# Products of 448 features as pairs of 64-row matmuls in two jobs, in a new order of all jobs

## The chip, the cores and the metric

The kernel runs on one core of a Trainium2 chip. Its engines work side by side: TensorE multiplies (PE in the profile, its weight loads PEld), VectorE (DVE) and ScalarE (ACT) do the elementwise work, GpSimd (POOL) some small things, and SyncE (SP) issues most of the DMAs. The metric is the device time of one execution in microseconds (us), the median of several runs.

## The reference, cut to what matters

```python
# x [2048, 448], H = 16 heads of 28, window W = 8 at dilation 2
h  = x + attention(layernorm(x) @ wqkv) @ wo      # each query sees 8 keys: pos, pos-2, .. pos-14
z  = gelu(layernorm(h) @ w_in)                    # [2048, 1792]
z1, z2 = z[:, :896], layernorm(z[:, 896:])
g  = w_sp @ z2 + b_sp[:, None]                    # [2048, 2048] times [2048, 896]
h2 = h + (z1 * g) @ w_out
```

All inputs and the result are bf16. Four of these products contract over 448 features: with wqkv (in the kernel qk and v), wo (y) and w_in (z1 and z2). 448 is three and a half times the 128 rows of TensorE.

## The kernel before

Every piece of work is a job of the `Planner`: a name, an engine, its operations with what they read and write, and a ticket for one or two of the eight PSUM banks where it needs them. `order` (line 301) doesn't plan. It puts the jobs in the order of the hand-written list ORDER (line 26), whose numbers are the jobs in the order of their creation, and gives each ticket the banks of the list BANK. `Sched.issue` (line 148) then goes through this order, works out which semaphores each operation has to wait for, and appends it to its engine's queue; every engine runs its own queue strictly in that order. A wait of TensorE on TensorE is left out there, since its matmuls end in order. So what is before what on one engine is read from ORDER alone, and the interleaving of different engines in it means nothing by itself. ON says which copies out of PSUM run on ACT, DVE or POOL.

The jobs on TensorE, by name:

- `warm`, the filler: one matmul of 256 columns on constant data. It stands in ORDER as many times as wanted, here only ahead of the first products.
- `xT0` to `xT3`: transposes of the first four normalised blocks of 128 tokens, copied out by `xe`. The other blocks are transposed by DMA.
- `qk t_g`: queries and keys of token range t (QT, two ranges of 256 tokens and three of 512) and head group g; weights `wqk`, which `wp` copies spread out of `wraw` (loads `wq_0` to `wq_4`), each head padded to 32 columns; copied out by `qe`.
- `v b`: values of two blocks of the attention; copied out by `ve`. 448 columns.
- `lg b_j`: logits of one block and half of the heads, 8 matmuls of 28 rows; `ex` takes the exponential on ACT, `mk` applies the mask on DVE.
- `o b`: probabilities times values, 16 matmuls of 29 columns; `rc`, `om`, `od` normalise, `oT` transposes by DMA.
- `y m`: the output projection of two token blocks; `h` adds it to x; `st1`, `mv1`, `rs1`, `n1` are the second layer normalisation, and `hT` transposes by DMA into hnT.
- `z2_m` (448 columns) and `z1_u` (512 columns): the two halves of the product with w_in; `z2c` copies raw, `z2g` and `z1g` take the gelu on ACT, and `st2`, `mv2`, `rs2`, `n2` normalise z2 on DVE and POOL.
- `g fc_tc_q`: four matmuls of 512 columns of the product with w_sp, of 16 that add up in one bank (line 958); `ua` and `um` on DVE add b_sp and multiply by z1.
- `wo m`: the product with w_out (line 982); `r` adds h on DVE and `out` stores. The last block, 15, is done in two halves of 224 columns.

The products with 448 features all go through `product` (line 485). It makes a job "F" (two, F0 and F1, for qk of the first range and for v0) of six matmuls with all 128 rows, three for each of two results in two banks (FK), and a job "H" of the half chunks (HK): one matmul with rows 0 to 63 for the first result and one with rows 64 to 127 for the second (`tile_position` (0, 0) and (64, 0)). The rows of the half chunk are taken so that the two matmuls lie on different rows and in different banks. F and H of one product stand anywhere in ORDER, in either order, and any of them may come first in its bank.

Of the kernel before, what the change touches and what calls it, by code (L numbers as in the profile page):

```python
# [6 lines left out]
D = 448  # L7
# [18 lines left out]
ORDER = [1, 25, 115, 26, 40, 2, 921, 921, 10, 921, 39, 30, 921, 921, 9, 31, 921, 921, 8, 27, 921, 41, 921, 5, 921, 43, 921, 6,  # L26
# [40 lines left out]
BANK = [2, 1, 5, 4, 0, 2, 6, 4, 6, 2, 0, 2, 4, 4, 2, 0, 0, 2, 4, 6, 6, 0, 4, 0, 4, 6, 4, 6, 0, 6, 7, 2, 0, 2, 2, 4, 6, 4, 3,  # L67
# [65 lines left out]
class Sched:  # L133
# [14 lines left out]
    def issue(self, exe, fn, reads=(), writes=(), dma=False):  # L148
# [23 lines left out]
        for e, c in sorted(needed.items(), key=lambda t: -t[1]):  # L172
# [8 lines left out]
            if c > myvc.get(e, 0):  # L181
                myvc[e] = c
# [138 lines left out]
def bass_sequential_preLN__sliding_local_dilated__mixer_gmlp__prompt_kernel(  # L321
# [17 lines left out]
    with contextlib.ExitStack() as top:  # L339
# [380 lines left out]
        def values(b):  # L720
# [12 lines left out]
            if b == 0:  # L733
                rd = [W_v + xh_res(k0, k0 + NK) for k0 in k0s]
# [320 lines left out]
```

## Time and profile before

| | |
|---|---|
| median of 3 runs | 240.5 us (240.25 to 240.63) |
| span of the profiled execution, first to last instruction | 238.8 us |
| TensorE busy | 232.1 us |
| DVE, ACT, POOL busy | 150.4, 91.6, 32.5 us |
| TensorE's first filler, first transpose, first product, first spatial matmul | at 1.51, 6.20, 8.88 and 118.16 us |

The profile is one execution of the program. Its own time outside of the profiler isn't known; the span leaves out what lies before the first and after the last instruction. Matmuls are pipelined: each row of TensorE has a modelled end, so rows overlap, and the distance from one start to the next is the better measure of what a matmul costs. A few records of matmuls are missing from the trace. In the rows below, L499 is the matmul of `product`, L797 the logits, L821 probabilities times values, L958 the spatial product, L982 the output, L660 the transposes and L997 the filler.

### The profile page before, as it was taken

What the parts mean: (1) busy time and instruction counts of PE and PEld (TensorE: products, weight loads), DVE (VectorE), ACT (ScalarE), POOL (GpSimd) and SP (SyncE); (2) the same over time, 40 slices, a digit from 0 to 9 for tenths busy, and PEclk for the clock granted to TensorE, in tenths of its full rate; (3) what the DMA queues carried; (4) which work ended last, traced back from release to release, by engine and by line L of the source; (5) the groups of instructions that cost most, each with busy time, mean ns of one, the idle gap of its engine ahead of it and who ended that gap; (6) DMA issues with size and microseconds to landing.
All of it is one profiled execution on the core that took longest, in us unless ns stands there. A gap on an engine that the chain in (4) does not pass through costs nothing.

```text
span 238.8 us, 4201 instructions
## 1 busy us (share of the span) xinstructions
PE 232.1 (97%) x1706; PEld 114.1 (48%) x1723; DVE 150.4 (63%) x321; ACT 91.6 (38%) x112; POOL 32.5 (14%) x75
## 2 busy tenths in 40 slices
PE   7899999999999999999999999999999999999995
PEld 5665445445455544444444444444444444444462
DVE  5899986999988985499985045024522514422863
ACT  3788487878889874679730000000000000000000
POOL 4450120320402121103242000000000000000000
DMA  5952424565852696999999990000000000003012
GB/s 139 337 166 55 91 53 91 137 170 148 112 103 47 119 149 133 186 148 200 192 235 182 160 198 3 0 3 0 0 0 21 3 0 19 0 3 115 19 58 77
DMA packets 66553, 23.10 MB, mean 97 GB/s; under 512 B 58726, under 2 KB 66406, under 8 KB 66534
## 3 DMA queue, kind: packets, MB, share of 16 engines
q1 hardware_dynamic: 66464, 22.83, 45.6%
q8 instruction: 13, 0.21, 0.4%
q14 instruction: 6, 0.05, 0.1%
q10 hardware_dynamic: 70, 0.00, 0.0%
HBM read 6.72 MB, written 1.84 MB: 36 GB/s over the span
## 4 chain that ended last, share of the span: by engine, by line
PE 94%; DMA 2%; SPq 1%; issue 1%; DVE 0%; DVEq 0%
PE psum L958 40%; PE psum L499 40%; PE psum L982 9%; PE psum L821 3%; PE psum L797 3%; DMA wraw<-in_A_wqkv_dram 2%; SPq L530 1%; DVE srg L989 0%; DVE wqk L515 0%; DVEq L203 0%
## 5 line engine op out<-in xcount | busy, mean ns | idle before, releaser
L967 DVE TENSOR_TENSOR ub<-psum,bb 128x512 bf16<-128x512 f32 x28 | 19.2, 690 | 53.8 <-PE psum L958 53.5
L958 PE MATMUL psum<-wsp_hi,z2p 128*128 128x512 bf16 x218 | 49.3, 379 | 0.3
L806 ACT ACTIVATE E<-psum 128x896 bf16<-128x896 f32 (+2 forms) x36 | 31.9, 928 | 6.8 <-PE psum L797 6.8
L958 PEld LDWEIGHTS psum<-wsp_hi,z2p 128*128 128x128 bf16 x224 | 21.9, 98 | 26.1
L499 PE MATMUL psum<-xhT,wqk 128*128 128x512 bf16 (+3 forms) x154 | 26.8, 336 | 1.0 <-issue 0.6
L958 PE MATMUL psum<-wsp_lb,z2p 128*128 128x512 bf16 x110 | 25.9, 379 | 0.2
L958 PE MATMUL psum<-wsp_la,z2p 128*128 128x512 bf16 x109 | 25.6, 379 | 0.3 <-issue 0.2
L499 PE MATMUL psum<-w_in,hnT 128*128 128x448 bf16 (+1 forms) x128 | 25.4, 353 | 0.1
L499 PE MATMUL psum<-hnT,w_in 128*128 128x512 bf16 (+1 forms) x112 | 24.4, 379 | 0.0
L982 PE MATMUL psum<-w_out,z1p 128*128 128x448 bf16 (+1 forms) x119 | 22.7, 341 | 0.0
L812 DVE TENSOR_TENSOR E<-E,maskb 128x1792 bf16<-128x1792 bf16 (+2 forms) x18 | 19.5, 1098 | 0.4 <-ACT E L806 0.4
L620 DVE BATCH_NORM_STATS2 st<-x_tm 128x6 f32<-128x448 bf16 x32 | 18.6, 608 | 1.7 <-DMA x_tm<-in_A_x_dram 1.6
L884 DVE BATCH_NORM_STATS2 st<-z2p 128x6 f32<-128x448 bf16 x32 | 18.4, 607 | 1.9 <-ACT z2p L877 1.6
L989 DVE TENSOR_TENSOR srg<-psum,x_tm 128x448 bf16<-128x448 f32 (+1 forms) x17 | 9.9, 594 | 13.2 <-PE psum L982 7.3
L499 PEld LDWEIGHTS psum<-xhT,wqk 128*128 128x128 bf16 (+1 forms) x160 | 12.3, 96 | 11.3 <-issue 2.5
L615 POOL TENSOR_TENSOR rs<-rs,negh 128x2 f32<-128x2 f32 (+1 forms) x21 | 17.2, 820 | 1.8
L958 PEld LDWEIGHTS psum<-wsp_lb,z2p 128*128 128x128 bf16 x112 | 10.9, 98 | 13.2
L958 PEld LDWEIGHTS psum<-wsp_la,z2p 128*128 128x128 bf16 x112 | 10.9, 98 | 13.4 <-DVE st L884 0.4
L925 ACT ACTIVATE z1p<-psum 128x1024 bf16<-128x1024 f32 x14 | 14.0, 1022 | 6.8 <-PE psum L499 6.8
L982 PEld LDWEIGHTS psum<-w_out,z1p 128*128 128x128 bf16 x119 | 11.6, 98 | 10.1
L499 PEld LDWEIGHTS psum<-w_in,hnT 128*128 128x128 bf16 (+1 forms) x128 | 10.3, 97 | 12.2 <-issue 3.2
L499 PEld LDWEIGHTS psum<-hnT,w_in 128*128 128x128 bf16 (+1 forms) x112 | 9.1, 96 | 11.2 <-issue 1.9
(54 smaller groups left out, 221.3 us busy)
## 6 DMA issues: line engine op xcount, KB each, us to landing
w_in<-in_B_w_in_dram SPq DMA_DIRECT2D x8, 224.0 KB, 3.0
out_dram<-srg SPq DMA_DIRECT2D x16, 112.0 KB, 1.7
x_tm<-in_A_x_dram SPq DMA_DIRECT2D x3, 448.0 KB, 5.9
w_out<-in_B_w_out_dram SPq DMA_DIRECT2D x1, 784.0 KB, 5.8
bb<-in_B_b_sp_dram SPq DMA_DIRECT2D x1, 512.0 KB, 5.5
wraw<-in_A_wqkv_dram SPq DMA_DIRECT2D x1, 448.0 KB, 4.7
wv<-in_A_wqkv_dram SPq DMA_DIRECT2D x2, 224.0 KB, 5.6
wo<-in_A_wo_dram SPq DMA_DIRECT2D x1, 336.0 KB, 5.8
```

The source lines that it names most:

```text
L499: ins = e.matmul(o, w, x, start=g not in seen, stop=left[g] == 0, **kw)
L615: (lambda e: e.tensor_tensor(R, A, negh[:, 0:1].to_broadcast([128, n]), ALU.pow), [rr, r_negh], r_rs[k][m:m + n])],
L620: [(lambda e: e.bn_stats(st[:, m, :], src), [rsrc], [r_st[k][m]])], dve_t(D))
L797: ins = e.matmul(psum[:, c:c + nq], qkT[p:p + DH, 2 * g + 1, k0:k0 + NK], qkT[p:p + DH, 2 * g, t0:t0 + nq], start=True, stop=True, tile_po ...
L806: return e.activation(o, i, AF.Exp, scale=SCALE)
L812: return e.tensor_tensor(a, a, maskb[:, 0:1, pad:pad + nq].to_broadcast([NK, NHEAD, nq]), ALU.mult)
L884: [(lambda e, m=m, k=k: e.bn_stats(st3[:, m, k, :], z2p[:, m, D * k:D * (k + 1)]), [r_z2[m]], [r_st[2][m]])], dve_t(D))
L925: return e.activation(o, i, AF.Gelu_apprx_tanh)
L958: ins = e.matmul(psv(tk), z2p[:, s, 128 * fc:128 * fc + 128], w[:, 512 * (tc % 2):512 * (tc % 2) + 512], start=(s == 0), stop=(s == NB - 1))
L967: [(lambda e, tc=tc, s=s, tk=tk: e.tensor_tensor(ub[:, s, :], psv(tk), bb[:, 512 * tc:512 * tc + 512], ALU.add), [r_bb], [r_ub[s]])], dve_ ...
L982: ins = e.matmul(psv(tk, 0, c1 - c0), z1p[:, fc, 128 * m:128 * m + 128], w_out[:, fc, c0:c1], start=(fc == 0), stop=(fc == FC7 - 1))
L989: [(lambda e, m=m, s=s, tk=tk, c0=c0, c1=c1: e.tensor_tensor(srg[:, s, c0:c1], psv(tk, 0, c1 - c0), x_tm[:, m, c0:c1], ALU.add), [r_x[m]], ...
```

## The change

`product` now makes fourteen matmuls of 64 rows for two results k of 448 features: the four chunks of the features are cut into lower (rows 0 to 63) and upper halves (64 to 127), three and a half chunks for each result. They are issued as pairs, a lower half for one result next to an upper half for the other. Job "A" holds four pairs, with the first result on the lower and the second on the upper rows; job "B" holds three pairs the other way round. A comes first, and B waits on TensorE's own semaphore for the end of A (`own`), since the two results change rows and both add up in the same banks. At least one other job of TensorE must lie between (`apart`).

```diff
+        def product(name, key, out, w, x, n, tk, reads, low=LOW, upp=UPP):
+            def pair(kl, ku):
+                return [e for a, b in zip([(kl, 0, c) for c in low[kl]], [(ku, 64, c) for c in upp[ku]]) for e in (a, b)]
+            first = [(0, 0, low[0][0]), (1, 64, upp[1][0])]
+            last = [(1, 0, low[1][-1]), (0, 64, upp[0][-1])]
+            def f(e, part):
+                for k, p0, c in part:
+                    ins = e.matmul(out(k), w(k, p0, c), x(k, p0, c), start=(k, p0, c) in first, stop=(k, p0, c) in last, tile_position=(p0, 0))
                 return ins
...
+            pa, pb = pair(0, 1), pair(1, 0)
+            ja = pl.job(name + "A", "pe", key, [(lambda e: f(e, pa), reads(pa), [])], 4 * half_t(n), acq=tk, kind="H")
+            jb = pl.job(name + "B", "pe", key, [(lambda e: f(e, pb), reads(pb), [])], 3 * half_t(n), acq=tk, kind="H")
+            pl.apart.append((ja, jb))
...
+LOW = [(0, 3, 2, 1), (0, 3, 1)]
+UPP = [(0, 3, 2), (0, 3, 1, 2)]
...
     def issue(...)
+        if own is not None:
+            waits.append(("pe", own))
...
     def order(self):
+        line = [j for j in out if j.eng == "pe"]
+        for a, b in self.apart:
+            between = line[line.index(a) + 1:line.index(b)]
+            assert between, ("no job between the two halves", a.name)
+            self.own[b] = a
```

ORDER, BANK and ON are new lists. Some dependencies that were written out (`after=` for logits, values, z1 and z2 and several loads, and `hold` for the loads of w_in) are gone; the lists alone set those orders now. TensorE's part of ORDER, written out by names up to the spatial product, before:

```
22*warm xT0 2*warm xT1 4*warm xT3 xT2 qk0_2F0 qk0_1F1 qk0_2F1 qk0_1F0 qk0_1H qk0_2H qk0_0H qk0_3H qk0_0F0 qk0_0F1
qk0_3F0 qk0_3F1 qk1_3F qk1_3H qk1_0H lg1_0 lg0_1 qk1_0F qk1_1F qk1_2F lg0_0 qk1_2H qk1_1H v0H v0F1 v0F0 lg1_1 lg2_0
v2F lg3_1 lg3_0 v2H v4F o0 o1 lg2_1 v4H qk2_0H qk2_0F qk2_3F qk2_2F qk2_1F qk2_2H v6H qk2_3H qk2_1H v6F o2 lg4_1 lg6_0
o3 qk3_3F lg4_0 lg5_1 qk3_3H qk3_2H qk3_2F lg5_0 lg6_1 qk3_1H qk3_1F v8F o5 o4 v8H y0H y0F lg7_1 lg7_0 qk3_0F lg8_0
lg8_1 qk3_0H qk4_0H qk4_0F o6 o7 qk4_1F lg10_0 lg10_1 qk4_1H y2H y2F v10H lg11_1 lg11_0 v10F o8 y4F lg9_1 lg9_0 y4H
qk4_2H qk4_2F lg12_1 lg12_0 qk4_3F o11 o9 o10 qk4_3H v16H v16F v12F lg13_1 lg13_0 v14H v12H v14F y6F lg15_0 lg14_1 y6H
z2_1H z2_1F o13 o12 z2_3H lg17_0 lg15_1 z2_3F y8F lg17_1 lg16_0 y8H z2_2H z2_2F z2_5H lg14_0 lg16_1 z2_5F o15 z1_0F
o14 z1_0H y10H z2_0H y10F z2_0F o17 o16 z1_1F z2_4F z1_1H z2_4H y12H y12F z1_2F z2_6F z2_6H z1_5H z2_7H z1_2H z1_5F
z2_7F z1_4F z1_6F y14F y14H z1_4H z1_6H z2_10H z2_10F z2_11F z1_9F z2_9F z2_13H z2_11H z2_9H z1_9H z2_13F z1_7F z2_12H
z2_8H z1_7H z1_8H z2_8F z1_8F z2_12F z1_12F z2_15F z1_12H z1_10H z2_14H z2_15H z1_10F z2_14F z1_11F z1_3F z1_13F
z1_11H z1_13H z1_3H g4_0_0 g3_0_0 g1_0_0
```

and after:

```
42*warm xT0 xT1 5*warm xT2 3*warm xT3 4*warm qk0_0A qk0_3A qk0_1A qk0_0B qk0_3B qk0_1B qk1_2A qk1_0A qk1_2B qk1_3A
qk0_2A qk1_0B qk0_2B qk1_1A qk1_3B qk1_1B lg0_0 v0A lg2_0 lg0_1 v0B v2A lg3_1 v2B lg3_0 lg2_1 v4A lg1_0 lg1_1 v4B
qk2_2A qk2_1A qk2_3A qk2_1B qk2_0A qk2_2B qk2_3B qk2_0B v6A o1 o0 lg4_0 lg4_1 v6B o2 qk3_2A lg6_1 lg5_0 qk3_2B qk3_3A
o4 lg5_1 lg6_0 o3 qk3_3B qk3_0A lg8_0 lg7_1 qk3_0B v8A qk3_1A lg8_1 lg7_0 v8B qk3_1B v10A o6 o5 v10B y0A lg9_1 lg9_0
y0B qk4_0A o7 lg11_0 lg10_1 o8 qk4_0B y2A lg12_1 lg10_0 y2B qk4_1A qk4_3A lg11_1 lg12_0 qk4_3B qk4_1B y4A qk4_2A y4B
qk4_2B v12A o10 o9 lg13_1 lg13_0 v12B o11 y6A lg14_0 lg15_1 y6B v14A lg15_0 v14B v16A lg14_1 lg16_0 v16B z2_0A o12 o13
lg17_1 z2_0B z2_1A lg17_0 lg16_1 z2_1B y8A z2_3A z2_2A z1_1A z2_3B y8B z2_2B z1_1B o14 o15 o16 o17 z2_4A z2_5A z2_4B
z2_5B y10A z1_0A y10B z1_0B z2_7A z1_4A y12A z2_7B y12B z1_4B z1_5A z2_6A z1_3A z2_6B z1_3B z2_9A z1_5B y14A z2_9B
y14B z2_8A z1_2A z1_6A z2_8B z1_2B z2_11A z1_9A z2_10A z2_11B z1_9B z1_6B z1_8A z1_7A z2_10B z1_7B z1_8B z2_13A z2_12A
z2_13B z2_14A z2_12B z2_14B z2_15A z1_10A z2_15B z1_12A z1_11A z1_13A z1_10B z1_13B z1_12B z1_11B g2_1_0 g3_0_0 g4_0_0
```

From there on TensorE has the same jobs g and wo in another order; before, the last were wo15 (two halves), wo12, wo14, wo13, and now they are wo13, wo12, wo14, wo15. SP's loads begin, before, with x0 x1 x2 wq_4 wq_3 wq_0 wq_1 wq_2 x4 wv_0 x8 wv_1 wo_1 wo_0 x12 wo_2, and after with x0 wq_4 x1 x2 x8 wq_1 x12 wq_3 wq_0 wq_2 x4 wo_2 wlo1 wv_1 wv_0; x8, x12, x4 and wq_0 have 448 KB each, x2 and the two wv 224, x0, x1, wq_1 and wq_4 112, wq_2 and wq_3 56. DVE casts wp0_0, wp2_0, wp3_1 first before, and wp3_1, wp0_0, wp4_2 after. Among the copies, z2c13 and ve12 go from DVE to ACT. In DVE's queue the normalisations n2_0 to n2_3 have two statistics (st2) of other blocks behind them after, and nine before.

More of the change, by code (lines that the diff above doesn't have):

```diff
@@ L146, in __init__, with issue @@
         self.store_keys = []
-    def issue(self, exe, fn, reads=(), writes=(), dma=False):
+    def issue(self, exe, fn, reads=(), writes=(), dma=False, own=None):
         prod, inc = exe, 1
@@ L233, in __init__ @@
         self.tickets = []
+        self.apart = []
         self.filler = None
@@ L292, in job @@
         return j
-    def hold(self, j, first):
-        if first not in j.deps:
-            j.deps.add(first)
-            j.ndep += 1
-            first.succ.append(j)
     def order(self):
@@ L756, in project @@
             tk = Ticket(2)
[L758 to L763 removed]
+            product("y%d" % m, key, lambda i, tk=tk: psv(tk, i, D), lambda i, p0, c, m=m: otv(64, p0, c, m + i),
+                    lambda i, p0, c: wo[p0:p0 + 64, c, :], D, tk, lambda part: r_wo2 + rot, LOWY, UPPY)
             pl.job("h%d" % m, "dve", kh,
@@ L800, in f @@
                     return ins
-                lgs[(b, j)] = pl.job("lg%d_%d" % (b, j), "pe", b + KEY["lg"], [(f, rq, [])], 0.2, acq=tk, kind="L", after=[o_jobs.get(b - NE)])
+                lgs[(b, j)] = pl.job("lg%d_%d" % (b, j), "pe", b + KEY["lg"], [(f, rq, [])], 0.2, acq=tk, kind="L")
                 def f2(e, nq=nq, j=j, slot=slot, tk=tk):
@@ L855, in bass_sequential_preLN__sliding_local_dilated__mixer_gmlp__prompt_kernel @@
         last_exp = exps[(NAB - 1, 1)]
-        gate = [lgs[(NAB - 1, 1)]]
         for m in range(NB):
             tk = Ticket(2)
-            def f(m=m, tk=tk):
-                return (
-                    [(k, psv(tk, k, D), hnT[:, m, FK[k][i], :], w_in[:, FK[k][i], FH + D * k:FH + D * (k + 1)], None)
-                     for i in range(3) for k in range(2)],
-                    [(k, psv(tk, k, D), hnT[p0:p0 + 64, m, c, :],
-                      w_in[p0:p0 + 64, c, FH + D * k:FH + D * (k + 1)], (p0, 0)) for k, (c, p0) in enumerate(HK)])
             kz = KEY["zr"] + KEY["zrs"] * m if RAW2[m] else KEY["z2"] + KEY["z2s"] * m
-            product("z2_%d" % m, kz, f, r_wi + [r_hn[m]], D, 6, tk, [] if RAW2[m] else gate)
+            product("z2_%d" % m, kz, lambda k, tk=tk: psv(tk, k, D), lambda k, p0, c, m=m: hnT[p0:p0 + 64, m, c, :],
+                    lambda k, p0, c: w_in[p0:p0 + 64, c, FH + D * k:FH + D * (k + 1)], D, tk, lambda part, m=m: r_wi + [r_hn[m]])
             def out2(m=m):
@@ L905, in bass_sequential_preLN__sliding_local_dilated__mixer_gmlp__prompt_kernel @@
             tk = Ticket(2)
-            def f(pair=pair, tk=tk):
-                return (
-                    [(i, psw(tk, i), w_in[:, c, 128 * fc:128 * fc + 128], hnT[:, 4 * tc:4 * tc + 4, c, :], None)
-                     for i, (fc, tc) in enumerate(pair) for c in FK[i]],
-                    [(i, psw(tk, i), w_in[p0:p0 + 64, c, 128 * fc:128 * fc + 128],
-                      hnT[p0:p0 + 64, 4 * tc:4 * tc + 4, c, :], (p0, 0)) for i, ((fc, tc), (c, p0)) in enumerate(zip(pair, HK))])
             rh = []
@@ L915, in bass_sequential_preLN__sliding_local_dilated__mixer_gmlp__prompt_kernel @@
                 rh += r_hn[4 * tc:4 * tc + 4]
-            product("z1_%d" % u, KEY["z1"] + KEY["z1s"] * u, f, r_wi + rh, 512, 6, tk, gate)
+            product("z1_%d" % u, KEY["z1"] + KEY["z1s"] * u, lambda i, tk=tk: psw(tk, i),
+                    lambda i, p0, c, pair=pair: w_in[p0:p0 + 64, c, 128 * pair[i][0]:128 * pair[i][0] + 128],
+                    lambda i, p0, c, pair=pair: hnT[p0:p0 + 64, 4 * pair[i][1]:4 * pair[i][1] + 4, c, :], 512, tk, lambda part, rh=rh: r_wi + rh)
             def f2(e, pair=pair, tk=tk):
@@ L927, in bass_sequential_preLN__sliding_local_dilated__mixer_gmlp__prompt_kernel @@
                    after=[last_exp], tbl="gelu")
-        for i, j in enumerate(j_win):
-            pl.hold(j, o_jobs[WINB + i])
-        load("bb", lambda: bb[:], lambda: B_b_sp.rearrange("(o n) -> o n", o=1).to_broadcast([128, S_TOK]), [r_bb], 0.6, (1.4, 3.2), key=28.0,
-             after=[o_jobs[NAB - 1]])
-        wl_ev = [o_jobs[min(b, NAB - 1)] for b in range(19)] + [j for j in ht_jobs for _ in range(2)]
-        late = ht_jobs[-1]
+        load("bb", lambda: bb[:], lambda: B_b_sp.rearrange("(o n) -> o n", o=1).to_broadcast([128, S_TOK]), [r_bb], 0.6, (1.4, 3.2), key=28.0)
         for s in range(NB):
@@ L1011, in bass_sequential_preLN__sliding_local_dilated__mixer_gmlp__prompt_kernel @@
                     reads += brs
-                key = sch.issue(j.eng, fn, reads, writes, dma=len(op) > 3)
+                key = sch.issue(j.eng, fn, reads, writes, dma=len(op) > 3, own=ends[pl.own[j]] if j in pl.own else None)
+                if j.eng == "pe":
+                    ends[j] = sch.cnt["pe"]
                 if j.name.startswith("out") or j.name == "touch":
```

86 lines of the change are left out of this document (25 added, 61 removed), and 100 rows, old and new, of tables (BANK, ON, ORDER).

## The prediction

> **What bounds the kernel now.** I read the head of the page and its chain of work first, then the waits of TensorE, then its timeline piece by piece.
>
> ```profile
> span 238.8 us, 4201 instructions
> ...
> PE 94%; DMA 2%; SPq 1%; issue 1%; DVE 0%; DVEq 0%
> ```
>
> ```profile
> PE psum L997 <- DVE warm L589: 1.5, 1, 1.5
> PE psum L499 <- issue: 0.6, 4, 0.2
> PE psum L660 <- DVE xn L631: 0.6, 2, 0.3
> PE psum L499 <- DVE wqk L515: 0.2, 1, 0.2
> PE psum L958 <- issue: 0.2, 1, 0.2
> ```
>
> The chain is TensorE's own work (94%). Its waits are over before 9.4 us, but for five of 0.16 us with no releaser, where the count of a row is one matmul short: a missing record and no wait. So from the first product to the last matmul the time is the sum of what TensorE executes, and only three things can move it: when the first product starts, what the stream costs, and what follows the last matmul. Next, the price of each kind, in start us, length, instruction, count:
>
> ```profile
> 86.54 0.38 PE L499 MATMUL psum<-hnT,w_in 64*128 64x512 bf16 x2
> 86.76 0.35 PE L499 MATMUL psum<-w_in,hnT 64*128 64x448 bf16 x2
> 86.95 1.78 PE L499 MATMUL psum<-hnT,w_in 64*128 64x512 bf16 x8
> 88.56 1.30 PE L499 MATMUL psum<-w_in,hnT 128*128 128x448 bf16 x6
> 89.70 2.75 PE L499 MATMUL psum<-hnT,w_in 128*128 128x512 bf16 x12
> 92.29 1.59 PE L499 MATMUL psum<-wo,OT 128*128 128x448 bf16 x8
> 93.72 0.59 PE L499 MATMUL psum<-hnT,w_in 64*128 64x512 bf16 x4
> 94.15 2.73 PE L499 MATMUL psum<-w_in,hnT 64*128 64x448 bf16 x14
> ```
>
> Starts count, since the lengths overlap. Six full matmuls of 448 columns last 88.56 to 89.70, 0.189 each; twelve of 512 last 2.59, 0.216 each. A pair of 64-row matmuls behind another pair costs the same as one full matmul: 0.22 for 512 columns (86.54 to 86.76), 0.19 for 448 (86.76 to 86.95). A change between full and half rows costs about 0.107: the eight at 92.29 are six full ones and a pair, seven passes or 1.32, and last 1.43; the eight at 86.95 are a pair and six full ones, 1.51, and last 1.61.
>
> ```profile
> 17.89 0.40 PE L797 MATMUL psum<-qkT 28*128 28x112 bf16 x16
> 18.22 1.31 PE L499 MATMUL psum<-wv,xhT 128*128 128x448 bf16 x6
> ...
> 21.23 0.95 PE L821 MATMUL psum<-V,E 128*128 128x29 bf16 x32
> 22.12 0.37 PE L797 MATMUL psum<-qkT 28*128 28x112 bf16 x8
> 22.42 0.36 PE L499 MATMUL psum<-wv,xhT 64*128 64x448 bf16 x2
> ```
>
> The logits are a third mode of 28 rows. Two jobs in a row (x16) take 0.33 us, and one alone (x8) takes 0.30: a run of logits costs some 0.33 whether it holds one job or two, and 0.10 more to enter it.
>
> **The change part by part.** *The products.* There are 67 of them. Each had six full matmuls and one pair; now it has seven pairs. Both are seven passes, and by the rows above a pass costs the same, so the stream itself gains and loses nothing: 89.1 us for the products (56 passes of 256 columns at 0.109, 182 of 512, 231 of 448), 96.7 for 448 spatial matmuls, 21.2 for the output, 7.3 for 18 attention jobs (0.40 each: 0.89 for two at 21.23 less a drain), 214.2 in all.
>
> *The changes of mode.* I wrote TensorE's part of ORDER out by job names, before and after. Before: 39 changes between full and half, and 19 runs of logits. After: 17, and 20 runs; the half rows stay set from one product to the next, and only attention jobs break them. So 22 changes go, 22 x 0.107 = 2.35 us, and one run comes, 0.33 + 0.10 = 0.43: **1.93 us less**. Check of the method on before, with the piece of the chain that holds the last matmuls:
>
> ```profile
> 228.04 7.98 PE psum L982 x49
> ```
>
> Started at 9.02 (worked out below), 214.2 + 39 x 0.107 + 19 x 0.43 ends at 235.6; the piece ends at 236.02, of which some 0.16 is the pipeline behind the last start of a matmul.
>
> *The head.* Now the start of the first product.
>
> ```profile
> 1.60:5.30 3.70, 3.70 (x18) 2.60 (x19) 1.00 0.75 174
> ```
>
> ```profile
> 1.51 4.48 PE L997 MATMUL psum<-warm 128*128 128x256 bf16 x22 [1.51 <-DVE warm L589]
> ...
> 6.43 0.38 PE L997 MATMUL psum<-warm 128*128 128x256 bf16 x2
> 6.65 0.39 PE L660 MATMUL psum<-ident,xn 128*128 128x128 bf16 x4
> 6.87 0.60 PE L997 MATMUL psum<-warm 128*128 128x256 bf16 x4
> ```
>
> ```profile
> 3.91 4.36 DMA wraw<-in_A_wqkv_dram
> ...
> 8.37 0.46 DVE wqk L515 x2
> ...
> 8.88 1.20 PE psum L499 x8
> ```
>
> ```profile
> 9.35 0.88 PEld L499 LDWEIGHTS psum<-xhT,wqk 128*128 128x128 bf16 x9 [0.25 <-DVE wqk L515]
> ```
>
> Before, the fourth load of wraw lands at 8.27, DVE spreads it, and the products start at 8.88; a weight load that waits at 9.35 costs about 0.14 more, hence 9.02. After, two things hold the start. First, 42 fillers stand ahead of the first transpose, not 22. In the first window of 3.7 us 18 start (0.206 each), later two take 0.22 (0.11 each). The 22 of before are issued by 5.83 (1.51 + 4.48 less the pipeline's 0.16); 20 more at 0.11 give 8.03, four transposes of 0.22 (6.65 to 6.87) and twelve more fillers 10.23. Second, SP issues x0, wq_4, x1, x2, x8, wq_1, x12, wq_3 and only then wq_0, the first 448 KB of the weights: 2072 KB up to it, where before 1176 KB were through with wq_1 at 8.27.
>
> ```profile
> 4.00:5.00 1.00, 1.00 (x7) 0.70 (x5) 0.73 (x3) 0.23 (x1) 0.62 (x2) 1.00 0.79 119
> 5.00:6.00 1.00, 0.99 (x7) 0.55 (x5) 1.00 (x5) 0.35 (x1) 0.39 (x2) 1.00 0.64 211
> ...
> 9.00:10.00 1.00, 1.00 (x9) 0.69 (x8) 1.00 (x5) 0.95 (x3) 0.00 (x0) 1.00 1.08 357
> ```
>
> The last column is GB/s. 896 KB more at 357 are 2.6 us: wq_0 at 10.8 if the queue flows as before. It moved only 330 KB from 4 to 6, and a queue that stays full would have moved some 714: 1.1 us less, 9.7. From landing to product took 0.6 with two casts on DVE; three stand ahead now, 0.8. So the start lies between 10.5 and 11.6, and I take the middle, 11.05: **2.03 us later**. It is no more than a middle: nothing in the trace says whether the slow stretch belongs to those two microseconds or to those loads.
>
> *The tail.*
>
> ```profile
> 232.07 0.39 DVE L989 TENSOR_TENSOR srg<-psum,x_tm 128x224 bf16<-128x224 f32 x1 [0.28 <-PE psum L982]
> ...
> 236.04 0.62 DVE L989 TENSOR_TENSOR srg<-psum,x_tm 128x448 bf16<-128x448 f32 x1 [0.70 <-PE psum L982]
> ```
>
> The last addition was one of 448 columns, 0.62; now wo15 comes last, whose second half takes 0.39: **0.23 us less**.
>
> *The added waits.* Each second job waits for the end of its first, and all of TensorE's queue stands behind it, then the copy out of its banks. In the tail DVE starts 0.02 us after the modelled end of the last matmul (236.02 to 236.04), some 0.37 after its start, and another matmul may start 0.19 after it. So 0.2 us of work between suffice. The least between is three pairs of 448 (0.57) or one logits job (0.30 beside two drains). I take 0; if this cover failed it would be up to 0.2 for each of 67, 13 us.
>
> *The other engines.* Copies move between ACT and DVE, loads move on SP, and some holds on loads go. TensorE never waits for them from 9.4 us on, and a later start gives them time. What is tight is the hand-over to the spatial stage.
>
> ```profile
> 90.00:100.00 10.00, 9.91 (x58) 4.43 (x56) 5.57 (x13) 4.75 (x6) 1.86 (x4) 1.00 0.81 159
> 110.00:120.00 10.00, 9.84 (x53) 4.24 (x51) 9.73 (x26) 7.93 (x10) 3.38 (x9) 1.00 0.99 194
> ```
>
> ```profile
> 115.37 1.77 DVE L893 TENSOR_SCALAR z2p<-z2p,mv,rs 128x896 bf16<-128x896 bf16 x4
> ...
> 117.17 1.10 DVE L884 BATCH_NORM_STATS2 st<-z2p 128x6 f32<-128x448 bf16 x2
> ```
>
> Before, the four normalisations that the first spatial jobs need were done at 117.14 for a start at 118.16, with nine statistics still to come. After, two come behind the last of these four: seven more go ahead, 7 x 0.55 = 3.9 us. DVE idles 4.4 us from 90 to 100 and can take them there. I put 0.3 us for all such waits, between 0 and 3.9.
>
> **Sum**, against the profiled span of 238.8: + 2.03 - 1.93 - 0.23 + 0.3 = + 0.17, a span of 239.0. The median of the runs, 240.5, is 1.7 over the span, and I keep that: **240.7 us**.
>
> **The rivals.**
> - *Faster: the queue stays full and nothing waits.* The start is bounded by the fillers, 10.23. + 1.21 - 1.93 - 0.23 gives 239.6. For: no wait in before once products run. Against: the slow stretch at 4 to 6 us.
> - *Slower: the weights land late.* wq_0 lands at 10.8, start 11.6: + 2.58 - 1.93 - 0.23 + 0.3, 241.2. It decides from a landing of about 10.6 on. For: it is the flow of before, unchanged; against: the early loads of x are large, and would fill the queue.
> - *Slower: the slow pace of the fillers lasts.* 20 of the 42 and the twelve behind them are counted at 0.11; if the 20 run at 0.21 as well, they cost 2.0 more, a start at 12.2: 241.5. By the Trainium skill ("TensorE: Matmul & The Clock Gate", Part 1: The HAM clock gate) the gate looks through a free-running window of about 3.4 us, so the change of pace may fall elsewhere in another run. The three runs of before, 240.25 to 240.63, show no such scatter, but they had few fillers behind it.
> - *Slower: the hand-over.* Half of the 3.9 us stays: 242.6.
> - *Slower: the added waits are not covered*, some 0.1 each: 247.
> - *Much slower: weight loads of the pairs are not hidden.*
>
> ```profile
> L499 PEld LDWEIGHTS psum<-w_in,hnT 64*128 64x128 bf16 x32 | 1.5, 94 | 2.4 <-issue 1.4 <-ACT z2p L880 0.4
> ```
>
> One load of 0.094 shown in each of 469 pairs is 44 us: 285. The pairs at 86.54 and 86.76, each behind another pair, speak against it, and so do the two pairs from 93.72, which take no more than 0.43. The Trainium skill (same page, Part 3, The mechanism) says that a weight load overlaps a running matmul only where the row group differs; read strictly it would give this rival, and these rows disagree. No run of more than four pairs is in the trace, though, and now there are dozens.
>
> **How the numbers follow.** The forecast, the middle start and small waits, has a chance of 0.40; the fillers alone 0.23; late weights 0.24; a lasting slow pace 0.04; the hand-over 0.05; uncovered waits 0.03; shown weight loads 0.01. A measurement of this kernel can tell 0.2% (0.48 us) from no change. Faster is 0.23, the same 0.40, slower 0.37. The range reaches from just below the bound of the fillers, 239.4, to 242.3, past the slow pace; it leaves out the last three rivals, 0.09, and some of each end.
>
> **What would show it.** Right: full-row matmuls of L499 gone; pairs at 0.19 and 0.22 from start to start in runs of any length; the first spatial matmul about 107 us after the first product (109 before); waits of TensorE of 0.2 to 0.5 us in all after the first product; the first product between 10.4 and 11.6. Wrong: pairs further apart than full matmuls were; waits of TensorE at each second job; an idle stretch ahead of L958; a first product before 10.2, or after 12.

## The result, and the profile after

The changed kernel takes **247.45 us** (median of 4 runs, 245.72 to 250.22) against 240.47 us of the kernel before beside it: 1.027 times, with a 95% interval of 1.023 to 1.031. The forecast was 240.7, which is no change that could be measured, and 242.3 at most; the kernel is 7 us slower. The profiled execution took 246.84 us, with a span of 245.1 where 239.0 was forecast. One run of the changed kernel (250.22) and one of list b below (246.06), both at a granted clock of 0.986, count as slow and stay out of the ratios; the changed kernel's median without it is 246.84.

The head of its page (the lines that were shown of before, and the row of the queue that carries instructions) and TensorE's waits, in us in total, times, longest:

```profile
span 245.1 us, 5072 instructions
...
q8 instruction: 17, 0.28, 0.5%
...
PE 81%; DMA 7%; ACT 5%; DVE 3%; SPq 2%; issue 1%; POOL 1%; DVEq 0%; POOLq 0%
```

```profile
PE psum L498 <- ACT E L786: 2.7, 2, 1.4
PE psum L962 <- DVE warm L582: 1.5, 1, 1.5
PE psum L498 <- ACT z2p L854: 0.9, 1, 0.9
PE psum L498 <- ACT z1p L895: 0.6, 1, 0.6
PE psum L947 <- DVE srg L954: 0.6, 1, 0.6
PE psum L498 <- DMA xhT<-xn: 0.6, 1, 0.6
PE psum L498 <- ACT wqk L508: 0.2, 1, 0.2
```

In this kernel L498 is the matmul of `product`, L786 the exponential, L854 and L895 the gelu of z2 and z1, L923 the spatial product, L947 the output, L954 the last addition. TensorE was 94% of the chain and is now 81%. Before, only one wait of any weight lay behind the first product's first weight load; now 5.4 us do. Its timeline shows that the rest came as forecast (start us, length, instruction, count):

```profile
11.03 6.34 PE L498 MATMUL psum<-xhT,wqk 64*128 64x256 bf16 x112 [0.15 <-ACT wqk L508]
...
107.34 3.19 PE L498 MATMUL psum<-hnT,w_in 64*128 64x512 bf16 x28
110.36 0.73 PE L498 MATMUL psum<-w_in,hnT 64*128 64x448 bf16 x6
...
112.23 4.89 PE L498 MATMUL psum<-w_in,hnT 64*128 64x448 bf16 x50
116.96 1.03 PE L498 MATMUL psum<-hnT,w_in 64*128 64x512 bf16 x8
```

The first product starts at 11.03 (forecast 11.05). Fourteen pairs of 512 columns take 107.34 to 110.36, 0.216 each; 25 pairs of 448 take 112.23 to 116.96, 0.189 each: the price of a full pass, in runs of any length.

To find where the time went I set the start of each of TensorE's jobs against the sum of the prediction's own price list (passes, 0.107 a change of mode, 0.43 a run of logits), begun at 11.03. Most of the way the two run side by side. They part by 6.5 us in all, and nearly all of it in seven steps, at the job that comes late each time (a step can be 0.2 longer than the idle time in the waits above, since the modelled end of a matmul lies behind the moment at which the next could start): v4 0.5 at 22.2 us, qk3_2 1.5 at 34.9, y8 1.0 at 74.5, z2_3 1.4 at 76.6, z2_5 0.8 at 84.8, a logits job 0.2 at 64.5, wo15 0.75 at 241.0. So 2.0 later at the head, 1.9 less for modes, 0.2 less at the tail and 6.5 of waits make 6.4 us; the two spans lie 6.3 apart.

**Three of the steps are ScalarE's tables.** Its timeline around them:

```profile
70.34 1.75 ACT L786 ACTIVATE E<-psum 128x912 bf16<-128x912 f32 x2 [0.21 <-PE psum L801]
72.11 1.28 ACT L854 ACT_TABLE_LOAD   x1
73.41 0.92 ACT L854 ACTIVATE z2p<-psum 128x896 bf16<-128x896 f32 x1
74.34 1.28 ACT L786 ACT_TABLE_LOAD   x1
75.64 0.93 ACT L786 ACTIVATE E<-psum 128x912 bf16<-128x912 f32 x1
...
82.44 1.28 ACT L895 ACT_TABLE_LOAD   x1
83.73 1.02 ACT L895 ACTIVATE z1p<-psum 128x1024 bf16<-128x1024 f32 x1
```

In the new list the gelu of z2_0 stands between two exponentials (ex16_0 ex17_1 **z2g0** ex17_0 z2c1 ex16_1). ScalarE changes its table of functions (ACT_TABLE_LOAD) to gelu, back, and later to gelu again: three loads of 1.28 us where before had one (at 75.67), and the jobs on TensorE that wait for these banks are y8, z2_3 and z2_5. The code's only guard, `after=[last_exp]`, holds a gelu behind ex17_1, and in this list ex17_1 isn't the last.

**The other three are DMAs that land late.** Pieces of the chain of work, in order of time:

```profile
17.65 4.40 DMA xhT<-xn
22.19 0.93 PE psum L498 x8
...
32.40 1.73 ACT E L786 x2
34.13 0.76 issue
34.89 1.04 PE psum L498 x8
...
233.81 3.98 DMA out_dram<-srg
...
238.53 1.67 DMA out_dram<-srg
240.33 0.64 DVE srg L954
241.01 1.53 PE psum L947 x14
```

A transpose took 4.40 us from issue to landing, a store 3.98 where another took 1.67. For qk3_2 the waits name ScalarE, but its exponentials end at 34.13 and it starts 0.76 later, with nothing shown between. What it waits for is xT9, the last transpose of its tokens. Queue q8 brings the engines their instructions, in packets of 16 KB; one packet is called a fetch below. With each DMA's issue and landing, and the packets of q8, all read out of the trace's records:

```
            issue   landing  latency   q8 packet
xT4         16.39   18.87    2.47      -
xT5         17.65   22.06    4.40      19.58 to 21.01
xT6         18.97   22.55    3.58      the same
xT7         21.48   23.95    2.48      -
xT9         30.46   34.69    4.23      32.49 to 33.54
a store     233.81  237.79   3.98      234.54 to 236.31
the next    238.53  240.20   1.67      -
```

Each late one in this table has a fetch between its issue and its landing. Not every slow transpose has: two others, issued at 24.75 and 27.90 behind loads of w_in and wo, took 3.88 and 3.64 us with no packet near, and TensorE didn't wait for them. The change makes more fetches: the trace has 2151 matmuls instead of 1706, and 17 packets instead of 13.

### The profile page after: what moved, and what is told of

Its sections match the earlier page's. It is cut to its first block, busy times and chain, and to the rows that moved or that the text cites. A ratio compares the mean times of both kernels' runs of the same rounds, so it can differ in the third digit from the quotient of the medians.

```text
span 245.1 us, 5072 instructions
## 1 busy us (share of the span) xinstructions
PE 235.5 (96%) x2151; PEld 119.0 (49%) x2151; DVE 147.5 (60%) x323; ACT 96.1 (39%) x117; POOL 33.9 (14%) x70
## 4 chain that ended last, share of the span: by engine, by line
PE 81%; DMA 7%; ACT 5%; DVE 3%; SPq 2%; issue 1%; POOL 1%; DVEq 0%; POOLq 0%
PE psum L923 39%; PE psum L498 32%; PE psum L947 6%; DMA x_tm<-in_A_x_dram 2%; PE psum L801 2%; DMA out_dram<-srg 2%; SPq L523 2%; PE psum L777 2%; ACT E L786 2%; DMA xhT<-xn 2%; DVE srg L954 1%; DVE st L613 1%; ACT L895 1%; ACT L786 1%; ACT L854 1%
## 5 line engine op out<-in xcount | busy, mean ns | idle before, releaser
L923 PE MATMUL psum<-wsp_hi,z2p 128*128 128x512 bf16 x224 | 50.1, 379 | 0.0
L923 PEld LDWEIGHTS psum<-wsp_hi,z2p 128*128 128x128 bf16 x224 | 21.9, 98 | 26.1
L786 ACT ACTIVATE E<-psum 128x896 bf16<-128x896 f32 (+2 forms) x36 | 31.7, 933 | 6.7 <-PE psum L777 6.2
L498 PE MATMUL psum<-xhT,wqk 64*128 64x512 bf16 (+1 forms) x280 | 26.7, 334 | 1.6 <-ACT E L786 1.4
L498 PE MATMUL psum<-w_in,hnT 64*128 64x448 bf16 x224 | 24.7, 350 | 1.8 <-ACT E L786 1.2
L923 PE MATMUL psum<-wsp_lb,z2p 128*128 128x512 bf16 x112 | 26.3, 379 | 0.0
L923 PE MATMUL psum<-wsp_la,z2p 128*128 128x512 bf16 x112 | 26.0, 379 | 0.0
L498 PE MATMUL psum<-hnT,w_in 64*128 64x512 bf16 x196 | 23.8, 376 | 0.0
L947 PE MATMUL psum<-w_out,z1p 128*128 128x448 bf16 (+1 forms) x119 | 22.7, 342 | 0.6 <-DVE srg L954 0.6
L613 DVE BATCH_NORM_STATS2 st<-x_tm 128x6 f32<-128x448 bf16 x32 | 19.1, 614 | 2.3 <-DMA x_tm<-in_A_x_dram 2.3
L608 POOL TENSOR_TENSOR rs<-rs,negh 128x2 f32<-128x2 f32 (+1 forms) x21 | 19.7, 939 | 1.8
L498 PEld LDWEIGHTS psum<-xhT,wqk 64*128 64x128 bf16 x280 | 13.3, 94 | 11.0 <-ACT E L786 2.0
L923 PEld LDWEIGHTS psum<-wsp_la,z2p 128*128 128x128 bf16 x112 | 10.9, 98 | 13.4 <-issue 0.4
L923 PEld LDWEIGHTS psum<-wsp_lb,z2p 128*128 128x128 bf16 x112 | 11.0, 98 | 13.1
L954 DVE TENSOR_TENSOR srg<-psum,x_tm 128x448 bf16<-128x448 f32 (+1 forms) x17 | 9.7, 593 | 12.5 <-PE psum L947 10.3
L947 PEld LDWEIGHTS psum<-w_out,z1p 128*128 128x128 bf16 x119 | 11.5, 98 | 11.2 <-DVE srg L954 1.0
L498 PEld LDWEIGHTS psum<-w_in,hnT 64*128 64x128 bf16 x224 | 10.5, 94 | 13.0 <-ACT E L786 1.7
L895 ACT ACTIVATE z1p<-psum 128x1024 bf16<-128x1024 f32 x14 | 14.0, 1022 | 4.7 <-PE psum L498 4.6
L508 ACT ACTIVATE qkT<-psum 128x1024 bf16<-128x1024 f32 (+1 forms) x17 | 13.4, 825 | 4.9 <-PE psum L498 4.9
```

What stands on the lines that cost most here:

```text
L498: ins = e.matmul(out(k), w(k, p0, c), x(k, p0, c), start=(k, p0, c) in first, stop=(k, p0, c) in last, tile_position=(p0, 0))
L508: j = pl.job(name, eng, key, [(lambda e: e.activation(o(), i(), AF.Copy) if eng == "act" else e.tensor_copy(o(), i()), list(reads), list(w ...
L608: (lambda e: e.tensor_tensor(R, A, negh[:, 0:1].to_broadcast([128, n]), ALU.pow), [rr, r_negh], r_rs[k][m:m + n])],
L613: [(lambda e: e.bn_stats(st[:, m, :], src), [rsrc], [r_st[k][m]])], dve_t(D))
L786: return e.activation(o, i, AF.Exp, scale=SCALE)
L895: return e.activation(o, i, AF.Gelu_apprx_tanh)
```

## The experiments

My theory was that the pairs do what they should, and that the new list of the order loses time in three ways: the gelu between exponentials, the later head, and transposes that are just in time and so pay for each fetch. The rivals: that the pairs themselves cost time, or that one loss hides the others. "Lost" below is TensorE's time from the first product to its end, less the sum of the price list, in the profiled execution.

| kernel | median us (range) | ratio to before, 95% | first product | lost |
|---|---|---|---|---|
| before | 240.05 to 242.2 in all its runs | | 8.88 | 0.3 |
| changed | 247.45 (245.72 to 250.22) | 1.027, 1.023 to 1.031 | 11.03 | 6.5 |
| full rows in the new order | 254.56 (254.20 to 255.64) | 1.059, 1.056 to 1.062 | 10.54 | 9.5 |
| pairs in the old order | 247.80 (247.61 to 249.07) | 1.030, 1.026 to 1.034 | 9.83 | 8.9 |
| gelu behind the exponentials | 245.33 (244.46 to 246.54) | 1.020, 1.016 to 1.024 | 11.19 | 4.0 |
| old head | 248.03 (247.53 to 249.31) | 1.032, 1.028 to 1.036 | 9.62 | 8.9 |
| wide fillers | 249.54 (248.50 to 251.29) | 1.037, 1.031 to 1.043 | 11.12 | 9.1 |
| before with wide fillers | 240.91 (240.17 to 243.03) | 1.001, 0.999 to 1.003 | 8.82 | 2.8 (the run of 243.03) |
| transposes first | 248.31 (248.19 to 248.58) | 1.032, 1.031 to 1.034 | 11.11 | 7.8 |
| head and gelu | 244.26 (241.89 to 244.92) | 1.011, 1.003 to 1.018 | 9.46 | 6.0 |
| new list a | 242.99 (241.09 to 244.48) | 1.009, 1.006 to 1.012 | 8.82 | 4.1 |
| new list b | 242.54 (241.93 to 246.06) | 1.008, 1.005 to 1.010 | 8.68 | 3.8 |
| new list c | 240.85 (240.28 to 241.94) | 1.001, 0.999 to 1.003 | 9.50 | 0.8 |
| new list e | 242.49 (241.99 to 243.38) | 1.010, 1.008 to 1.012 | 8.86 | 3.3 |

**Full rows in the new order.** The pairs alone undone.

```diff
-            pa, pb = pair(0, 1), pair(1, 0)
+            full, half = ([(0, 2, 3), (0, 1, 3)], [(1, 0), (2, 64)]) if low is LOW else ([(0, 1, 2)] * 2, [(3, 0), (3, 64)])
+            pa, pb = [(k, -1, c) for k in range(2) for c in full[k]], [(k, half[k][1], half[k][0]) for k in range(2)]
```

(p0 of -1 stands for all 128 rows.)

> The changed kernel's order with products as the kernel before makes them: six matmuls of 128 rows in the first job, two of 64 rows side by side in the second. The changes of mode rise from 17 to 62. Theory (pairs save 0.107 us a change and cost nothing): 45 x 0.107 = 4.8 us more, 252.2 us (251.5 to 253.0). Rival (pairs cost something too, by more weight loads or by more instructions to fetch: 2151 matmuls instead of 1706): 250.5 us or less, with the transposes near 19 and 32 us landing 2.5 us after their issue.

7.1 us more, above both ranges. From the first product to its end TensorE takes 7.8 us more. By the price list 45 changes of mode are 4.8 of it, and 3.0 is lost in waits; the start is 0.5 earlier. The price can be read in this trace itself:

```profile
105.91 2.75 PE L500 MATMUL psum<-hnT,w_in 128*128 128x512 bf16 x12
108.60 0.36 PE L500 MATMUL psum<-w_in,hnT 64*128 64x448 bf16 x2
108.80 0.38 PE L500 MATMUL psum<-hnT,w_in 64*128 64x512 bf16 x2
109.11 1.31 PE L500 MATMUL psum<-w_in,hnT 128*128 128x448 bf16 x6
```

Twelve full matmuls of 512 columns are 2.59 and last 2.69 up to the first pair; the pair of 512 is 0.216 and lasts 0.31 up to the next full one. Over the whole trace a change takes 0.096 us from full to half rows (median of 21 without a wait) and 0.106 back (of 26), so 45 are some 4.5. In this order the first half is six passes, so the banks behind it come free later, which its waits show:

```profile
PE psum L500 <- ACT E L788: 3.0, 8, 0.9
PE psum L500 <- ACT z2p L856: 1.8, 2, 1.2
```

The rival, that pairs cost something, named 250.5 or less and falls. The price of a change holds, but not that nothing else moves.

**Pairs in the old order.** The other way round: `product` as changed, with ORDER, BANK and ON of before, its names mapped and 17 jobs moved by a few places so that one lies between each A and B.

```diff
-ORDER: ... v0H v0F1 v0F0 lg1_1 ...
+ORDER: ... v0A (a neighbouring job) v0B lg1_1 ...
```

> Products as pairs, but in the order, the banks and the engines of the kernel before; where both halves of a product would stand side by side on TensorE (17 products), one neighbouring job is put between. Theory (the halves need an order of their own: a half of 4 passes where one of 1 pass stood, and the other of 3 where one of 6 stood, so all that stands between them and their evacuation comes later): first product at 9.5 us, waits of TensorE for banks and evacuations of 7 to 9 us spread over 15 to 125 us in pieces of 0.2 to 0.9, none for a table load; 246 to 248.5 us. Rival (only the new order is at fault, pairs fit any order): 238.5 to 240.5 us.

247.80, in the theory's range, with 8.9 us lost. The waits are of many kinds (DMA of hnT, ScalarE and VectorE), with one of 2.0 where the theory had pieces of 0.9 at most; the trace is of the slowest run, 249.07. So pairs do need an order of their own. The new list wasn't needless, it was loose.

**Gelu behind the exponentials.**

```diff
-RAW2 = [0, 1, 2, ...        ACT: ex16_0 ex17_1 z2g0 ex17_0 z2c1 ex16_1 ...
+RAW2 = [1, 1, 2, ...        ACT: ex16_0 ex17_1 z2c0 ex17_0 z2c1 ex16_1 z2g0 ...
```

> The first gelu (z2_0) no longer stands between exponentials: ScalarE copies z2_0's product at that place and takes its gelu behind the last exponential; all else as in the changed kernel. Theory (table loads): one ACT_TABLE_LOAD between 60 and 90 us instead of three, the waits of y8, z2_3 and z2_5 (1.04 + 1.40 + 0.77 = 3.2 us) gone, time 247.45 - 3.2 = 244.2 us, range 243.6 to 245.0. Rival (ScalarE has more work than this stage holds, and now an extra copy of 0.8 us): TensorE still waits 2 us or more for ScalarE there, time 246.3 or more.

One load is left in that stage, and y8, z2_3 and z2_5 wait no more; ScalarE's timeline:

```profile
74.65 0.95 ACT L775 ACTIVATE E<-psum 128x912 bf16<-128x912 f32 x1
75.61 1.28 ACT L840 ACT_TABLE_LOAD   x1
76.91 0.95 ACT L840 ACTIVATE z2p<-z2p 128x896 bf16<-128x896 bf16 x1
```

The time fell by 2.1 (1.5 from 246.84), not 3.2: three other jobs now wait, qk4_0 0.5, y12 0.3 and z2_11 0.9. The mechanism is shown; what it is worth in the whole kernel is half to two thirds of the waits that it removes.

**Old head, and wide fillers.** The first takes back the order of the first nine loads and the fillers of before; the second only halves the number of fillers and doubles their columns.

```diff
-SP: x0 wq_4 x1 x2 x8 wq_1 x12 wq_3 wq_0 wq_2 x4 ...     PE: 42*warm xT0 xT1 5*warm xT2 3*warm xT3 4*warm
+SP: x0 x1 x2 wq_4 wq_3 wq_0 wq_1 wq_2 x4 x8 x12 ...     PE: 22*warm xT0 2*warm xT1 4*warm xT2 xT3
```

> The changed kernel with the order of the first nine loads and the fillers (22, 2, 4) of the kernel before. Theory (the new head costs what it moves): first product at 9.0 to 9.6 us instead of 11.03, the rest as in the changed kernel, time 245.4 to 246.1 us; the runs lie closer together than 245.7 to 250.2. Rival (the head's gain is given back): x rows 8 to 15 come later, the transposes too, and TensorE waits for them between 14 and 40 us: time 247.0 or more.

```diff
-e.matmul(psv(tkw, 0, 256), warm[:, 256:384], warm[:, 0:256], ...)      # 54 in ORDER
+e.matmul(psv(tkw, 0, 512), warm[:, 256:384], warm[:, 0:512], ...)      # 27 in ORDER
```

> The changed kernel with 27 fillers of 512 columns instead of 54 of 256: the same time on TensorE, 27 matmuls fewer in its instruction stream ahead of the first product; nothing else. Theory (transposes that are in flight while a 16 KB packet of instructions is fetched land 1 to 2 us late): first product still at 11.0 us; every packet comes 0.5 to 2.5 us later than 15.2, 19.6, 32.5, 38.5 us and so on, since fewer matmuls stand ahead of it; other transposes are late (latency 3.4 to 4.4 instead of 2.5 us, each with a packet between its issue and its landing), so the waits near 22, 35 and 241 us change in size by up to 1.5 us each, others come, and the time moves by 0.5 to 3 us, more likely up than down. Rival (the late transposes are late for their place on SP's queue or for other loads): the same transposes stay late by the same amounts, the time stays within 0.5 us of 247.45.

The old head starts 1.4 us earlier and the time doesn't fall. Its rival's number came, but not for its reason: between 14 and 40 us TensorE waits 1.5 us, less than the 2.0 of the changed kernel, and what is new lies at 48 us (0.8), at 114 (0.5) and in the tail (1.6 instead of 0.6). The wide fillers show why. With nearly the same start (11.12) and the same list the kernel is 2.1 us slower, and all that differs is that 27 matmuls fewer stand in the instruction stream. The packets come at 15.7, 21.6, 32.6 and 40.1 us instead of 15.2, 19.6, 32.5 and 38.5; xT5 takes 2.49 now and v4 no longer waits, xT7 takes 4.21 and qk2_2 waits 1.0, and in the tail wo15 waits 1.9 instead of 0.6. The chain of this kernel:

```profile
20.40 4.21 DMA xhT<-xn
24.61 0.14 issue
24.74 6.98 PE psum L497 x64
```

The old head has 28 fillers, so its packets fall at the same places of the instruction stream as those of the wide fillers do: these two are the pair to compare, 248.03 and 249.54. The difference of 1.5 us is the distance of their first products. With four runs each, whose ranges overlap, that the head is worth just this is likely and not shown.

**Before with wide fillers.** The same edit in the kernel before (28 fillers to 14).

> The kernel before with 14 fillers of 512 columns instead of 28 of 256: the same time on TensorE, 14 matmuls fewer ahead of the first product, so that every packet of instructions is fetched at another place of its order. Theory (the old order has slack ahead of its transposes: there, packets between the issue and the landing of a transpose are met with banks and work that wait for nothing): the time stays within 0.5 us of 240.5, while transposes with a packet between issue and landing still take 3.4 to 4.5 instead of 2.5 us. Rival (the old order is fast because its packets happen to fall where no transpose is in flight): 1.5 to 3 us more, as the wide fillers brought the changed kernel.

240.91, within its uncertainty the same. Its profiled execution is the slowest of its ten runs, 243.03: ten transposes with a packet in flight took 3.7 to 4.7 us, VectorE waited 1.5 us for one of them at 48 us and TensorE 1.1 us behind it, and 2.8 us were lost in all. The median hardly moves, though. So the old order isn't proof against the packets, but in most executions it has the slack, and that it was fast is no accident of where the packets fall.

**Transposes first.**

```diff
-SP: xT7 wlo7 w_in0_1 xT10 w_in0_0 wo_1 wo_0 xT11 xT8 xT9 w_in2_1 wlo0 oT1 oT0 wlo5 ...
+SP: xT7 xT10 xT11 xT8 xT9 wo_1 wo_0 oT1 oT0 ... oT6 w_in0_1 w_in0_0 w_in2_1 ... hT4 wlo7 wlo0 wlo5 ...
```

> The changed kernel with the loads w_in0_0, w_in0_1, wo_0, wo_1 and a transposed load taken from between the transposes xT7 to xT9 on SP's queue and put behind them. Theory (order of SP): xT9 lands 3 to 5 us before 34.69, the wait of 1.49 us at 34.89 goes, time 245.9 us (245.5 to 246.3). Rival (whatever transposes are in flight when a 16 KB packet of instructions is fetched land 1 to 2 us late): the packet stays at 32.5 us, another transpose is late for it, and the time is 246.8 to 247.8.

The waits of v4 and qk3_2 went, and the time didn't fall: others came behind (z2_11 0.8, y12 0.3), and in the profiled execution something that I had not expected. The windows of three stretches around 75 us (stretch, PE busy, PEld, DVE, ACT, POOL, then the granted clock, DMA share, GB/s):

```profile
71.00:75.30 4.30, 2.05 (x34) 0.87 (x34) 0.28 (x3) 4.26 (x5) 1.09 (x3) 1.00 0.58 122
75.40:78.70 3.30, 3.30 (x20) 1.39 (x18) 3.30 (x5) 1.39 (x2) 0.00 (x0) 0.50 0.25 36
78.80:82.00 3.20, 3.20 (x40) 1.53 (x37) 2.58 (x4) 1.72 (x2) 0.00 (x0) 1.00 0.83 134
```

After the two waits for table loads TensorE's clock is halved for 3.4 us, 20 matmuls where the next stretch has 40: 1.7 us more in this execution. Two of the four executions show no such stretch (granted clock 1.000) and are no faster, with spans of 246.5 and 246.7 against 246.5 and 246.9; what they lose in its place isn't known.

**Head and gelu together**, with 56 fillers of 128 columns, so that about as many matmuls stand ahead of the products and the packets stay at their places in the stream.

> The changed kernel with two of the parts undone together: z2_0's gelu behind the last exponential, and the first nine loads and the fillers' time of the kernel before; the fillers are 56 of 128 columns, so that about as many matmuls stand ahead of the products (56) as in the changed kernel (54). Theory (the losses add up: head 1.5 us, as between the two kernels with 27 and 28 fillers; gelu 2.1 to 3.2; the rest, some 2 us, is transposes that are late for packets of instructions, and stays): 247.45 - 1.5 - 2.1 to 3.2 = 242.8 to 243.9 us, TensorE's waits behind the first product 2.5 to 4.5 us. Rival (one loss hides another, as a transpose waited for is late anyway): 245 us or more.

244.26, between theory and rival: of the 3.6 to 4.7 us expected 3.2 came (2.6 from 246.84). The four runs lie 3.0 us apart, so the losses add up for the larger part, and closer than that it can't be said. In the profiled execution (244.74) 6.0 us are lost still, most of it behind transposes and loads: v0 (0.8), v4 (0.8) and z2_11 (1.1) start 0.04 to 0.14 us after the landing of a load of wv and of two transposes, which took 5.1 and 4.7 us with a packet in flight.

**New lists.** If only the order is at fault, there must be one for pairs that loses nothing. I searched one with a model of the five queues, fed with the durations of these traces, a table load of 1.28, and fetches at six positions that delay what is in flight.

```diff
-ORDER = [25, 40, 1, 9, 41, 30, ...        BANK = [0, 2, 3, 2, ...
+ORDER, BANK: new lists of the same jobs; z2_0 copied raw as above
```

> Pairs, z2_0 copied and its gelu behind the last exponential, the first nine loads and the fillers of the kernel before, and a new list of the order of all engines and of the banks: the list was searched with a model of the five queues made of the durations in these traces, with the gelu switch priced at 1.28 us and transposes in flight at a fetch of instructions landing 1.1 us after it, for six positions of the fetches. 19 changes of mode. Theory (pairs save their changes of mode, what was lost is the order's): first product at 9.5 to 9.8, TensorE's waits behind it 3 us or less, time 238.5 to 241 us. Rival (waits that come from the pairs themselves): 243 us or more.

> As the kernel beside it, another list from the same search: 17 changes of mode, and fewer transposes that are just in time. Theory: 238.5 to 241 us; rival: 243 us or more. By the model this one is 0.4 us slower at the fetches' likeliest position and depends less on where they fall.

242.99 and 242.54: 4.5 to 4.9 us better than the changed kernel, but over the theory's range by 1.5 to 2, and the first stands at the rival's bound of 243. The traces name what is lost, and it is again DMAs that are just in time, loads of wv in both, transposes in the first (1.3) and a load of w_in in the second:

```profile
PE psum L486 <- DMA w_in<-in_B_w_in_dram: 1.4, 1, 1.4
PE psum L486 <- DMA wv<-in_A_wqkv_dram: 0.9, 1, 0.9
```

So the third keeps the first 16 loads of before and reckons later loads longer.

> As the two lists before it, with the first 16 loads in the order of the kernel before (the halves of wv ahead of x rows 8 to 15, no transposed load of the spatial weights among them), later loads reckoned a microsecond longer, and the list searched again. 19 changes of mode, 21 runs of logits. Theory (pairs can be used without loss once no transpose and no load is just in time): the wait of 1.25 to 1.4 us of v0 at 16 us goes, no wait over 0.6 us is left, time 239.0 to 241.0 us. Rival (something in the pairs costs time that the model hasn't): 242 us or more.

240.85, which is the kernel before within the interval (0.999 to 1.003), with a span of 238.6. Its waits, all of them; the first and the fourth lie ahead of the products, and the second ends with the first product:

```profile
PE psum L950 <- DVE warm L570: 1.5, 1, 1.5
PE psum L486 <- DVE wqk L496: 0.7, 1, 0.7
PE psum L486 <- DMA xhT<-xn: 0.4, 1, 0.4
PE psum L641 <- DVE xhT L496: 0.3, 1, 0.3
PE psum L911 <- issue: 0.2, 1, 0.2
```

With 469 pairs and 67 waits of B for A, TensorE waits 0.6 us behind the first product. That settles the pairs: neither they nor their waits cost time that the sum doesn't hold.

> As the third list, searched further: 18 changes of mode and 21 runs of logits, first product at 9.1 to 9.6 us; by the model 0.4 us less than the third list, and 0.7 us less where the packets fall worst. Theory (with no wait left, the pairs give what their 21 changes of mode fewer save, 2.2 us, less two more runs of logits, 0.9, less some 0.5 at the head): 239.6 to 240.4 us, 0 to 0.4% under the kernel before. Rival (the old order has nothing left to gain, its changes of mode are hidden somewhere): 240.6 us or more.

242.49. The rival's number came again without its reason: a fetch at 19.3 us held up a transpose (4.46 us), and the job behind it waited 1.1. The model doesn't place fetches well enough to order lists that lie within a microsecond. No version that was run beats the kernel before.

## Why the prediction was wrong

- *What bounds the kernel now*: right. That is also where the trap was: with no wait in before, every wait in after is new, and I had no row of it.
- *The products*, the same seven passes: right, 0.216 and 0.189 in runs of 14 and 25 pairs. The rival of weight loads that aren't hidden falls. With it falls the strict reading of the Trainium skill ("TensorE: Matmul & The Clock Gate", Part 3, The mechanism), by which a weight load overlaps a running matmul only where the row group differs. Here the row groups repeat from pair to pair, and a pair costs no more than a full pass.
- *The changes of mode*, 1.93 less: right. Starts follow the sum between waits, and changes that were put back cost 0.096 to 0.106 each, for 0.107 reckoned.
- *The head*, + 2.03: right, 11.03 for 11.05, wq_0 landing at 10.23 in the middle of the bounds. The slow pace of the fillers, a rival, added little: the 42 were issued by 8.24, for 8.03 reckoned. What the head is worth in time isn't shown closer than that 1.5 us fits.
- *The tail*, 0.23 less: right for the last addition (0.39); that the stores of the four slots of `srg` could hold up the addition ahead of wo15 was not seen.
- *The added waits*, 0: right, with list c the proof. The rival that put 0.1 us on each of the 67 named 247 us, and 247.45 came; that is luck, since TensorE waits six times behind the first product, each time at a first job.
- ***The other engines*, + 0.3, is the step that failed: it measured 6.5.** "TensorE never waits for them from 9.4 us on, and a later start gives them time" took a property of before's order for one of the kernel. In the new order TensorE waits for ScalarE's tables, for late transposes and for a store. I had written out TensorE's part of the new list by names and counted its changes, but read VectorE's part only for the hand-over, and ScalarE's and SP's hardly at all. The gelu among the exponentials stood in the list for anyone to read, and 1.28 us a load stood in before's trace: two more loads, 2.6 us, and the waits that they cause came to 3.2. That wo_0, wo_1 and two loads of w_in stood between the transposes stood there too.
- The hand-over, the one place that I called tight, didn't wait at all: the first spatial matmul comes 112.7 us after the first product (forecast 107), by the waits ahead of it.
- The range gave 3.9 us to these waits at most, and only to a single rival of 0.05. It was the widest unknown of the sum, and its price should have been the range.

Some of the 6.5 us could not have been read: where a packet is fetched, and that this delays a transpose. But before's trace had such cases (oT2 3.94 us, oT5 4.18, against 2.4 to 2.5), and the spread of these latencies asked for slack.

## What to carry to other kernels

Where a change replaces an order, write out every engine's part of it and not only the bound one's; count the switches of function on ScalarE and mark each load or transpose that lands less than 2 us before its first use (with a packet in flight they came 1.1 to 2.3 us late in the table above). An order in which nothing waits can be worth more than the work that is saved: here 1.93 us of changes of mode, against 6.5 us of waits. Compare versions with equally many instructions ahead of the stage in question, or the fetches may decide.

## What the hardware showed

**Fetches delay DMAs.** In the 14 profiled executions, transposes of one block (xT and oT) with no other kind of DMA in flight ahead took 2.45 us (median of 111; nine in ten under 2.6) where no 16 KB packet of q8 was in flight with them, and 3.95 us (median of 60; nine in ten over 3.0) where one started within 2.2 us of their issue. That it is the packet, the wide fillers show: as the packets moved, xT5 went from 4.40 to 2.49 us and xT7 from 2.48 to 4.21. A packet lasts some 0.9 to 2.0 us and comes every 125 to 130 matmuls (17 for 2151, 13 for 1706). Why it holds up the others was not tried.

**The clock can fall after short waits.** With the transposes first, two waits of 1.0 and 1.2 us within 3.4 us were followed by 3.41 us at half clock. By the Trainium skill ("TensorE: Matmul & The Clock Gate", Part 1: The HAM clock gate) the gate judges free-running windows of 3413 ns and halves the clock after an idle one. The length agrees, but TensorE wasn't idle: it had been busy 1.17 of the 3.41 us before the fall. The changed kernel has the same two waits (0.9 and 1.2), at full clock. The records of the clock say what differs. In the 12 traces that hold such records, every change lies a whole number of times 3.413 us behind the first one (in the run above 20 and 21 times), and of the traces with these two waits only the run above has both of them whole within one stretch of that grid. The stretches with the least work that no fall followed have 1.49, 1.55 and 1.57 us busy (wide fillers, full rows in the new order, old head), and the changed kernel's 1.91.

So a wait of a microsecond may cost 1.7 more, and by these traces its place in the grid decides, which begins at another time in each (4.5 to 7.1 us). With the gelu moved, two executions had spans of 242.7 and 242.8 at a mean clock of 1.000, and two of 244.4 and 244.8 at 0.993 and 0.992, which fits one such stretch. The changed kernel's four spans, 244.0 to 248.5, lie between 244.0 and 245.1 when 1.7 is taken off for each stretch that their mean clocks stand for. The kernel before, with its 0.3 us of waits, shows 0.998 to 1.000 in all its runs. The fall was seen in one trace and is argued for the executions without a trace; against it stand the four executions with the transposes first, where those at full clock are no faster.
